# Recurrent retention and a channel mix on one core: block 2's layout, the place of the value weights, and a new order of pieces

## The chip, the core and the metric

The kernel runs on one core of a Trainium2 chip. Five engines work side by side, each through its own queue in order: TensorE (PE, matrix products; its weight loads are shown as PEld), VectorE (DVE), ScalarE (ACT), GpSimd (POOL) and SyncE (SP). Transfers are issued from the queues of POOL, SP and ACT and carried by 16 DMA engines. The metric is the time of one execution in microseconds on the device; lower is better. A profile is one execution taken by the hardware profiler.

## The reference, cut to what matters

Inputs: q, k, v of shape (4, 8, 768, 64): 4 batches, 8 heads, 768 tokens, 64 numbers a head. Then the weights of a channel mix, with 512 columns in and out and 1024 inside. All float32.

```python
# part 1, retention, each batch and head by itself
for t in range(S):
    state = gamma * state + outer(k[t], v[t])
    y[t] = scale * (q[t] @ state)
# part 2, with x = the heads of y side by side, 512 numbers a token
x_prev = x one token earlier (zero for the first)
xk = mu_k * x + (1 - mu_k) * x_prev
xr = mu_r * x + (1 - mu_r) * x_prev
k = max(xk @ w_k, 0);  v = k * k @ w_v
out = sigmoid(xr @ w_r) * v
```

## The kernel before, in words

The 768 tokens of a batch are cut into 3 blocks of 256, so there are 12 blocks, numbered 0 to 11; block n belongs to batch n // 3. Within a block the recurrence is done as products: scores of keys against queries, masked to be causal, times the values (inside the block), plus the queries times a carried state (from the blocks before). Each block's result is then mixed with its shifted self and goes through three projections.

The order of all work is written out by hand in one string, ORDER (lines 24 to 80). Each word is a piece: a code, numbers (block first, then parts), after "@" the PSUM banks that it writes, after "~" the engine (v DVE, a ACT, p POOL, s SP; pieces of TensorE have none). The kernel walks through the words and issues each at once, so the string sets the order of every engine's queue. The waits between engines follow from the tiles that the pieces share. Nothing is moved by a planner afterwards.

The codes that matter here (functions in brackets):

- lq, lk, lv (load): block n's q, k, v from memory; lq.0.0.2 is the part of block 0 for heads 0 to 3. POOL's loads of q and k turn float32 into float16. wk.h, wv.h, wr (load_wk, load_wv, load_wr): the projections' weights, wk and wv in two halves.
- cq, ck (cast): the first halves of block 0's q and k, loaded by SP as float32, to float16. vs (scale_v): v with the decay of each token.
- Tq, Tk (trans): transposes of q and k on TensorE. Eq, Ek (turned_q, turned_k): their copies out of PSUM.
- S (scores), M (masked, on DVE); C (state), U (summed), G (decayed): the carried state. I (inter_off) and J (inter_on): queries times carried state. Y (intra): masked scores times values.
- D (yout): result of a block to x transposed. dx (differ), t (weighed) and X (mixed): xk and xr (X.n.0.j and X.n.1.j, j a quarter of the 512).
- K (keys), Qa (relued), Qb (squared): first projection, its max with 0, its square. R (gate), s (opened): the sigmoid's projection, the sigmoid. V (values), O (result), st (store): second projection, product with the sigmoid, and the store of 128 tokens. V.n.tb.half reads half of wv. Vc, Oc and sc do the last 128 tokens in two column halves.
- z.c: products of zeros on TensorE that nobody reads. cm (masks), gy (powers), mu, mt, me: constants.

How a block's 256 tokens lie over partitions depends on the lists at the top. Blocks in HALF (6 to 11) use 64x64 tiles of TensorE. Blocks in WIDE (2 to 5, line 22) and HALF load k and v in two transfers of 128 tokens, 64 numbers a run (line 229); the others load 256 tokens in one transfer, two neighbouring tokens a run of 128 numbers (line 234). For WIDE blocks, scores take 64x128 tiles (line 330), the state and the values 128x64 tiles (lines 383 and 477). Blocks in neither list take 64x64 tiles for all three (lines 338, 394 and 488), twice as many products. Blocks in WHOLE (0 to 3) are transposed in 128x64 tiles (line 271), the others in 64x64 (line 277).

Two pieces of TensorE recur 120 times in all and are of one size, four products of 512 columns or eight of 256: K (48 pieces), R (24) and V (46, and two pieces Vc of the same length).

Buffers are rings: 4 for q and k in float16 and for v, 3 for masked scores and mixed inputs. A load waits until the block that held its buffer is done with it.

Of the kernel before, what the change touches and what calls it, by code (L numbers as in the profile page):

```python
# [34 lines left out]
X.1.1.1~v Qa.1.0~a t.0.1.0~a K.1.2@7 I.2@23 Qb.0.1~a Qa.1.1~a wv.0~p Qb.0.2~a Tq.4@01 Eq.4~a Y.2
Qa.1.3~a Qb.1.1~a X.0.1.3~v X.1.1.3~v R.1.1@4 Tk.4@01 Ek.4~a J.2 R.1.0@6 Qa.1.2~a s.1.0~a X.0.1.2~v
X.0.1.1~v X.0.1.0~v R.0.1@5 s.0.1~a s.1.1~a R.0.0@7 s.0.0~a S.4.1@01 Qb.1.0~a D.2~v dx.2~v X.2.0.2~v
X.2.0.0~v S.4.0@23 Tq.3@4 Eq.3~a X.2.0.1~v wv.1~p X.2.0.3~v Tk.3@7 lq.5~p Ek.3~a K.2.2@5 Qa.2.2~a
K.2.3@4 M.4.1~v M.4.0~v Qa.2.3~a Qb.2.3~a lk.6~p S.3.1@67 M.3.1~v S.3.0@01 vs.3~p C.3@23 U.3.0~a
Qb.2.2~a K.2.1@4 Qa.2.1~a K.2.0@2 Qa.2.0~a I.3@45 lq.6~p vs.4~v C.4@67 U.3.1~v X.2.1.1~v V.0.1.0@3  # L40
M.3.0~v V.1.0.0@2 G.3~a U.4.0~v I.4@01 X.2.1.3~v U.4.1~v J.3 Qb.1.3~a Y.4 Qb.2.0~a lk.5~p X.2.1.2~v
X.2.1.0~v Y.3 D.3~v dx.3~v V.0.0.0@7 V.0.1.1 O.0.1~v Tq.5@45 J.4 D.4~v dx.4~v R.2.0@6 Qb.2.1~a
V.0.0.1 O.0.0~v X.3.0.1~v Eq.5~a Qb.1.2~a V.1.0.1 X.3.0.2~v O.1.0~v Tq.6@01 Eq.6~a Tk.6@45 Ek.6~a
st.0.0~s lk.7~p st.1.0~s V.1.1.0@3 V.1.1.1 O.1.1~v s.2.0~a R.2.1@0 s.2.1~a lv.5~p X.3.0.0~v
X.3.0.3~v Tk.7@67 Ek.7~a G.4~a S.6@45 M.6~v Tk.5@23 Ek.5~a vs.5~v V.2.0.0@0 K.3.2@1 Qa.3.2~a K.3.0@6
S.5.0@23 M.5.0~v S.5.1@45 C.5@1 U.5.0~v K.3.3@7 Qb.3.2~a Qa.3.0~a lq.7~p K.3.7@6 Qa.3.3~a Qa.3.7~a
lv.6~p lq.8~p vs.6~v M.5.1~v V.2.0.1 st.0.1~s I.5@67 O.2.0~v st.2.0~s C.6@23 U.6.0~a U.6.1~v U.6.2~v
K.3.6@1 Qa.3.6~a lk.9~p X.3.1.3~v Y.5 Tq.7@45 Eq.7~a U.6.3~v X.3.1.2~v I.6@01 J.5 X.3.1.0~v D.5~v
X.3.1.1~v Qb.3.3~a G.6~a V.2.1.0@2 K.3.1@3 V.2.1.1 O.2.1~v Qb.3.7~a Qa.3.1~a Qb.3.1~a dx.5~v K.3.4@4
K.3.5@5 Qa.3.5~a X.5.0.0~v X.5.0.3~v R.3.1@2 s.3.1~a lv.7~p Qa.3.4~a X.5.0.1~v Qb.3.4~a R.3.0@5  # L50
R.4.0@2 s.3.0~a s.4.0~a Qb.3.0~a X.5.0.2~v vs.7~v K.5.2@4 S.7@67 st.1.1~s M.7~v Qb.3.5~a Y.6
Qb.3.6~a lv.10~p C.7@23 U.7.0~v X.5.1.1~v Qa.5.2~a K.5.0@5 R.4.1@6 Qa.5.0~a D.6~v s.4.1~a V.4.0.0@4
V.4.0.1 V.3.1.0@5 U.7.1~v Qb.5.0~a X.5.1.3~v U.7.2~v I.7@01 X.5.1.2~v U.7.3~v Tq.8@67 Eq.8~a
X.5.1.0~v O.4.0~v lv.8~p vs.8~v Qb.5.2~a lq.10~p lk.8~p Tk.8@23 Ek.8~a V.3.1.1 V.3.0.0@4 C.8@67
O.3.1~v st.2.1~s st.3.1~s Y.7 dx.6~v D.7~v Tq.10@23 V.3.0.1 Eq.10~a G.7~a dx.7~v X.6.0.2~v V.4.1.0@5
V.4.1.1 X.6.0.0~v R.5.0@0 R.5.1@1 K.5.3@2 Qa.5.3~a Qb.5.3~a O.3.0~v s.5.0~a K.5.1@4 X.6.0.1~v lq.9~p
lk.10~p Qa.5.1~a Qb.5.1~a lv.11~s s.5.1~a X.6.0.3~v K.6.3@2 Qa.6.3~a K.6.2@3 K.6.5@4 Qa.6.2~a
U.8.0~v Qa.6.5~a X.6.1.2~v V.5.0.0@0 st.3.0~s X.6.1.0~v K.6.4@1 Qa.6.4~a O.4.1~v U.8.1~v X.6.1.1~v
U.8.2~v I.8@45 S.8@67 Tk.10@23 Ek.10~a V.5.0.1 lv.9~p X.6.1.3~v vs.9~v K.6.6@1 Qb.6.2~a M.8~v
Qa.6.6~a Qb.6.5~a S.10@67 O.5.0~v Y.8 M.10~v D.8~v vs.10~v dx.8~v st.5.0~s st.4.0~s Tk.9@23 Ek.9~a  # L60
V.5.1.0@1 V.5.1.1 X.8.1.3~v vs.11~v O.5.1~v lk.11~p Qb.6.3~a Tk.11@23 Qb.6.4~a X.8.0.1~v X.8.0.3~v
lq.11~p Tq.11@67 Ek.11~a X.8.1.2~v Tq.9@45 Eq.9~a K.6.1@0 Qa.6.1~a Eq.11~a R.6.0@2 s.6.0~a K.6.7@4
R.6.1@5 s.6.1~a Qa.6.7~a C.9@23 S.11@67 X.8.0.0~v C.10@01 K.6.0@5 U.9.0~a Qa.6.0~a Qb.6.0~a U.9.1~v
X.8.0.2~v Qb.6.6~a U.9.2~v U.9.3~v G.9~v Qb.6.1~a R.7.0@4 s.7.0~a K.8.1@5 Qa.8.1~a K.8.0@3 Qa.8.0~a
# [733 lines left out]
```

## Time and profile before

| What | us |
|---|---|
| median of 3 runs | 154.2 (153.81 to 154.3) |
| the profiled execution, whole | 154.38 |
| its span, first to last instruction | 152.6 |
| PE busy | 144.1 |
| DVE busy | 128.7 |
| ACT busy | 100.6 |
| POOL busy | 55.3 |

The span is what the trace shows; the whole execution has some 1.8 us around it. In the views that follow, a row of the chain of waits has start, length and what was done then. A row of a timeline has start, length, engine, line, operation and tiles. A row of transfers has the tiles, the issuing queue, the count, the size and the median time from issue to landing. Rows of groups have busy time and mean length of one, then the engine's idle time before them. A row of windows has the stretch, its length, then for PE, PEld, DVE, ACT and POOL the busy time with the count of instructions, the granted clock, the DMA share and GB/s.

### The profile page before, as it was taken

To read this page: it belongs to the slowest core of one execution; us is meant where nothing else is said; L and a number is where in the kernel's file an instruction comes from. 1 tells how busy PE (TensorE), PEld (TensorE's weight loads), DVE (VectorE), ACT (ScalarE), POOL (GpSimd) and SP (SyncE) were. 2 spreads that over 40 slices of the span, in tenths; PEclk is the share of its full clock that TensorE was granted. 3 is DMA by queue.
4 is the path that set the end of the run, shared out by engine and by line. 5 is a ranking of instruction groups with operands and counts; after the bars stand their busy time and mean duration, and the time that the engine had idled before them with its cause. 6 is when DMAs were issued, how large, how long until landed. Compare 5 with 4: busy or idle time off the path is not lost.

```text
span 152.6 us, 5532 instructions
## 1 busy us (share of the span) xinstructions
PE 144.1 (94%) x2426; PEld 82.9 (54%) x2426; DVE 128.7 (84%) x214; ACT 100.6 (66%) x187; POOL 55.3 (36%) x65
## 2 busy tenths in 40 slices
PE   7977799999999999999999999899999999999990
PEld 3354487758655554547554655557555445744450
DVE  7876999999999999999999999999789999702240
ACT  3466979899934894979483889879405048997130
POOL 7954988579867109997600000000000000000000
PEclk9999999999999999999999999999999999999999
DMA  5999999999999999999999203220002050010435
GB/s 137 215 224 200 207 229 194 170 249 210 196 167 207 236 250 112 290 275 203 206 191 225 83 0 136 81 73 0 4 4 75 0 205 1 14 54 4 158 117 206
DMA packets 45624, 22.16 MB, mean 145 GB/s; under 512 B 37400, under 2 KB 41248, under 8 KB 45600
## 3 DMA queue, kind: packets, MB, share of 16 engines
q0 software_dynamic: 38704, 14.42, 74.0%
q1 hardware_dynamic: 6592, 7.21, 13.7%
q8 instruction: 19, 0.31, 0.8%
q10 hardware_dynamic: 304, 0.18, 0.5%
q14 instruction: 5, 0.04, 0.1%
HBM read 24.16 MB, written 6.29 MB: 200 GB/s over the span
## 4 chain that ended last, share of the span: by engine, by line
PE 91%; DVE 3%; ACT 2%; issue 1%; DVEq 0%
PE ps L623 27%; PE ps L581 14%; PE ps L611 14%; PE ps L571 14%; PE ps L701 4%; PE ps L277 3%; PE ps L440 2%; PE ps L271 2%; DVE a L353 2%; PE ps L330 1%; PE ps L477 1%; ACT qT L240 1%; PE ps L317 1%; PE ps L461 1%; PE ps L641 1%; PE ps L365 1%
## 5 line engine op out<-in xcount | busy, mean ns | idle before, releaser
L623 PE MATMUL ps<-wv,k2s 128*128 128x512 f16 x184 | 43.3, 380 | 0.0
L590 ACT ACTIVATE kr<-ps 128x512 f32<-128x512 f32 x48 | 27.4, 596 | 21.5 <-PE ps L581 11.1
L623 PEld LDWEIGHTS <-k2s 128*128 128x128 f16 x184 | 17.0, 98 | 19.3 <-ACT k2s L602 0.2
L629 DVE SCALAR_TENSOR_TENSOR os<-ps,rs 128x512 f32<-128x512 f32 x23 | 15.5, 685 | 12.4 <-ACT rs L617 7.1
L611 PE MATMUL ps<-wr,xr 128*128 128x512 f16 x96 | 23.5, 379 | 0.0
L581 PE MATMUL ps<-xk,wk 128*128 128x256 f16 x192 | 23.4, 273 | 0.0
L571 PE MATMUL ps<-xk,wk 128*128 128x512 f16 x96 | 22.9, 379 | 0.0
L229 POOL DMA_DIRECT2D k<-in_k_dram x20 | 17.9, 908 | 11.1 <-PE ps L383 6.8
L581 PEld LDWEIGHTS <-wk 128*128 128x128 f16 x192 | 18.3, 98 | 4.4 <-issue 0.2
L240 ACT COPY qT<-ps 128x1024 f16<-128x1024 f16 (+1 forms) x13 | 12.4, 951 | 9.2 <-PE ps L277 7.8
L557 DVE SCALAR_TENSOR_TENSOR xr<-dx,mu,xT 128x256 f16<-128x256 f32 (+1 forms) x32 | 18.0, 579 | 0.1
L617 ACT ACTIVATE rs<-ps 128x512 f32<-128x512 f32 x24 | 13.7, 594 | 6.1 <-DVE os L629 3.2
L229 POOL DMA_DIRECT2D v<-in_v_dram x18 | 16.0, 904 | 3.6 <-DMA wr<-in_moe_w_r_dram 1.9
L557 DVE SCALAR_TENSOR_TENSOR xk<-dx,mu,xT 128x256 f16<-128x256 f32 (+1 forms) x32 | 17.1, 581 | 0.2
L353 DVE TENSOR_TENSOR a<-ps,c_sb 128x1024 f16<-128x1024 f32 (+1 forms) x14 | 14.6, 1066 | 0.7 <-PE ps L338 0.4
L602 ACT ACTIVATE k2s<-kr 128x512 f16<-128x512 f32 x24 | 14.6, 626 | 0.2
L571 PEld LDWEIGHTS <-wk 128*128 128x128 f16 x96 | 9.1, 98 | 10.3
L611 PEld LDWEIGHTS <-xr 128*128 128x128 f16 x96 | 9.1, 98 | 10.2 <-DVE xr L557 0.3
L598 ACT ACTIVATE k2s<-kr 128x512 f16<-128x512 f32 x24 | 14.4, 625 | 0.3
L240 ACT COPY kT<-ps 128x1024 f16<-128x1024 f16 (+1 forms) x13 | 12.3, 944 | 2.9 <-PE ps L271 2.0
L528 DVE TENSOR_TENSOR dx<-xT 128x1024 f32<-128x1024 f32 x11 | 13.5, 1223 | 0.3
L252 DVE TENSOR_TENSOR vs<-v,csm_sb 128x1024 f16<-128x1024 f32 x10 | 12.2, 1219 | 0.2 <-DMA v<-in_v_dram 0.2
(74 smaller groups left out, 165.5 us busy)
## 6 DMA issues: line engine op xcount, KB each, us to landing
out_dram<-os SPq DMA_DIRECT2D x23, 256.0 KB, 3.0
v<-in_v_dram POOLq DMA_DIRECT2D x18, 256.0 KB, 7.3
q<-in_q_dram POOLq DMA_DIRECT2D x11, 256.0 KB, 7.8
k<-in_k_dram POOLq DMA_DIRECT2D x21, 128.0 KB, 8.9
v<-in_v_dram POOLq DMA_DIRECT2D x2, 512.0 KB, 7.1
wk<-in_moe_w_k_dram POOLq DMA_DIRECT2D x2, 512.0 KB, 11.2
wv<-in_moe_w_v_dram POOLq DMA_DIRECT2D x2, 512.0 KB, 9.7
wr<-in_moe_w_r_dram POOLq DMA_DIRECT2D x1, 512.0 KB, 9.3
```

The source lines that it names most:

```text
L229: e.dma_start(out=dst[:, :, i * D : i * D + D], in_=src[:, i * P : i * P + P].rearrange("h p d -> p h d"),)
L240: e.copy(out=out, in_=in_)
L353: nc.vector.tensor_tensor(out=a_full(n)[:, i, :, j0:j1], in0=pairs(banks("S", n, i, j0))[:, :, j0:j1], in1=(below if wide(n) else causal[: ...
L557: nc.vector.scalar_tensor_tensor(out=XM[w](k)[:, j, t0:t1], in0=DX(k)[:, j, t0:t1], scalar=mu[:, w * NCO + j : w * NCO + j + 1], in1=x[:, ...
L571: nc.tensor.matmul(banks("K", n, g), lhsT=wk16[:, co, g * P : g * P + P], rhs=XM[0](k)[:, co, :], start=(co == 0), stop=(co == NCO - 1),)
L581: nc.tensor.matmul(pz[:, i, :], lhsT=wk16[:, co, fo * P : fo * P + P], rhs=XM[0](k)[:, co, m * TM + t0 : m * TM + t1], start=(i == 0 and c ...
L590: nc.scalar.activation(out=kr, in_=banks("K", n, g, *u), func=AF.Relu)
L598: nc.scalar.activation(out=k2s[:, n % 3 : n % 3 + 2, g, :], in_=kr, func=AF.Square,)
L602: nc.scalar.activation(out=K2(n)[:, w * g : w * g + w, t0:t1], in_=kr.rearrange("p a t -> p (a t)").rearrange("p (i t) -> p i t", i=w), fu ...
L611: nc.tensor.matmul(banks("R", n, tb), lhsT=XM[1](k)[:, co, t : t + P], rhs=wr16[:, co, :], start=(co == 0), stop=(co == NCO - 1),)
L623: nc.tensor.matmul(banks("V", n, tb), lhsT=K2(n)[:, fo, tb * P : tb * P + P], rhs=wv16[:, fo, :], start=(fo == 0), stop=(fo == NFO - 1),)
L629: nc.vector.scalar_tensor_tensor(out=OS(2 * n + tb), in0=banks("V", n, tb), scalar=1.0 / (KSC * KSC), in1=RS(2 * n + tb), op0=ALU.mult, op ...
```

## The change

Five things change; all but two are in the string ORDER.

1. Block 2 leaves the list WIDE. Its k and v come in one transfer each, and its scores, state and values take 64x64 tiles: 32 score products instead of 16, 16 state products instead of 8, and 32 value products instead of 16.
2. The masks' constants are made in three parts at three places (cm.0, cm.1, cm.2) instead of all at the start.
3. On POOL's queue, q of block 2 stands ahead of wk, and wv.0, wr and wv.1 stand ahead of or among the loads of block 4 and ahead of those of block 3. Before, both parts of wv stood behind them.
4. Some pieces change engine: the first casts of block 0 and one eviction of its k go from ACT to DVE, vs.3 from POOL to DVE, U.0.0 from DVE to ACT.
5. All pieces stand in another order, with other PSUM banks. Of the products of zeros, four pieces of z.2 (eight products) are gone. Both transposes of block 2 stand ahead of the first K piece; before, Tq.2 stood behind the fourth. V pieces of blocks 0 and 1 come much earlier, and the first two stores with them.

```diff
-WIDE = (2, 3, 4, 5)
+WIDE = (3, 4, 5)
...
-cm gy.0~v mu~a lv.0~p lq.0.0.2~s lk.0.0.2~s ck.0.0.2~a cq.0.0.2~a z.12@6 Tq.0.0.2@0 Tk.0.0.2@1 gy.1~v
-z.1@2 mt@2 Ek.0.0.2~a Eq.0.0.2~a S.0.1.0.2@01 S.0.0.0.2@45 me~a lk.0.2.4~p Tk.0.2.4@2 Ek.0.2.4~a
-lq.0.2.4~p vs.0~v C.0@67 U.0.0~v Tq.0.2.4@3 Eq.0.2.4~a lq.1~p lk.1~p M.0.1.0.2~v z.2@2 S.0.1.2.4@23
-U.0.1~v lv.1~p lk.2~p I.0@01 S.0.0.2.4@67 M.0.0.2.4~v wk.0~p wk.1~p G.0~a z.2@6 Tq.1@6 Eq.1~a vs.1~p
-lq.2~p Tk.1@7 Ek.1~a M.0.0.0.2~v M.0.1.2.4~v Y.0 D.0~v t.0.0.3~a t.0.0.2~a t.0.0.1~a lv.2~p z.2@4
-S.1.1@23 M.1.1~v C.1@01 U.1.0~v z.2@4 I.1@23 S.1.0@67 X.0.0.1~v t.0.1.2~a X.0.0.2~v Tk.2@0 t.0.1.3~a
-t.0.0.0~a M.1.0~v X.0.0.0~v z.2@4 Y.1 t.0.1.1~a X.0.0.3~v Ek.2~a K.0.0@0 K.0.1@6 lq.4~p U.1.1~v
-G.1~a wr~p lk.4~p D.1~v dx.1~v X.1.0.2~v X.1.0.0~v K.0.2@1 Qa.0.0~a Qb.0.0~a Qa.0.2~a lq.3~p
...
+lv.0~p lk.0.2.4~p mu~a gy.0~v cm.2~v lq.0.2.4~p lq.0.0.2~s cq.0.0.2~v cm.0~v z.12@6 Tq.0.0.2@0
+Eq.0.0.2~a lk.0.0.2~s ck.0.0.2~v Tk.0.0.2@1 Ek.0.0.2~a mt@0 S.0.0.0.2@23 cm.1~v Tk.0.2.4@1 lq.1~p
+vs.0~v C.0@45 gy.1~v Tq.0.2.4@6 Eq.0.2.4~a M.0.0.0.2~v me~a U.0.0~a Ek.0.2.4~v U.0.1~v G.0~a
+S.0.1.0.2@23 M.0.1.0.2~v lk.1~p lv.1~p S.0.0.2.4@67 Tq.1@4 Eq.1~a I.0@01 S.0.1.2.4@23 lk.2~p lq.2~p
+M.0.0.2.4~v Tk.1@5 M.0.1.2.4~v Y.0 D.0~v Ek.1~a t.0.0.3~a S.1.0@23 M.1.0~v Tk.2@5 t.0.0.0~a wk.0~p
+wk.1~p lv.2~p vs.1~p C.1@01 U.1.0~v z.1@6 I.1@23 X.0.0.0~v t.0.0.2~a t.0.0.1~a S.1.1@67 wv.0~p wr~p
+Tq.2@0 X.0.0.1~v M.1.1~v z.2@4 Y.1 t.0.1.3~a Eq.2~a X.0.0.3~v t.0.1.0~a X.0.0.2~v D.1~v dx.1~v
+X.1.0.1~v X.1.0.2~v K.0.1@0 Ek.2~a K.0.0@6 X.1.0.0~v X.1.0.3~v Qa.0.0~a vs.2~v Qa.0.1~a Qb.0.1~a
+Qb.0.0~a U.1.1~v lq.4~p K.0.2@2 K.0.3@3 X.0.1.0~v X.1.1.3~v lk.4~p Qa.0.2~a Qb.0.2~a G.1~a K.1.2@0
+K.1.0@2 Qa.1.0~a S.2.0@67 M.2.0~v C.2@1 U.2.0~v V.0.1.0@5 Qa.1.2~a t.0.1.1~a X.1.1.0~v X.1.1.2~v
+t.0.1.2~a X.0.1.2~v K.1.3@4 Qa.1.3~a I.2@01 S.2.1@67 M.2.1~v V.0.0.0@2 K.1.1@4 X.1.1.1~v Qb.1.3~a
+Tq.4@67 X.0.1.3~v X.0.1.1~v Y.2 Qa.0.3~a D.2~v dx.2~v Qb.1.2~a Eq.4~a X.2.1.1~v X.2.0.0~v Qb.0.3~a
+X.2.1.2~v X.2.0.3~v Qa.1.1~a Qb.1.1~a R.0.0@3 s.0.0~a X.2.1.3~v X.2.0.1~v R.0.1@6 Qb.1.0~a s.0.1~a
+wv.1~p X.2.0.2~v Tk.4@01 R.1.0@4 R.1.1@3 s.1.1~a V.0.1.1 O.0.1~v st.0.1~s lv.3~p vs.3~v V.0.0.1
+O.0.0~v s.1.0~a Ek.4~a st.0.0~s K.2.2@4 K.2.1@5 Qa.2.1~a S.4.1@01 M.4.1~v Qa.2.2~a S.4.0@67 lk.3~p
+lq.3~p X.2.1.0~v C.3@23 U.3.0~a U.3.1~v Tk.3@5 Ek.3~a Tq.3@4 K.2.3@0 Eq.3~a lv.4~p M.4.0~v K.2.0@1
+vs.4~v Qa.2.3~a Qb.2.3~a Qa.2.0~a S.3.0@67 S.3.1@45 M.3.1~v Qb.2.2~a I.3@23 G.3~a V.1.0.0@0 V.1.0.1
+M.3.0~v O.1.0~v R.2.1@4 s.2.1~a C.4@67 U.4.0~v Y.3 lv.5~p lk.5~p Tk.5@45 vs.5~v I.4@01 J.3 V.1.1.0@6
+V.1.1.1 D.3~v dx.3~v lk.7~p Y.4 Qb.2.1~a Qb.2.0~a C.5@2 Ek.5~a Tk.7@45 Ek.7~a U.4.1~v G.4~a J.4
+D.4~v dx.4~v X.3.0.0~v R.2.0@3 s.2.0~a X.3.0.1~v V.2.0.0@7 lq.5~p lq.7~p Tq.7@01 Eq.7~a Tq.5@45
...
+Qa.5.3~a Qb.5.1~a V.4.0.0@1 V.4.0.1 Tk.9@23 Tk.8@45 lk.10~p Tk.10@67 lv.9~p V.5.1.0@0 Qb.5.3~a
...
-    def masks(e):
+    def masks(e, part):
         for out, col, op in (
-            (ident, 0, ALU.is_equal), (causal[:, 0], 1, ALU.is_ge), (causal[:, 1], 1, ALU.is_gt),
-            (step, 2, ALU.is_ge), (below, 0, ALU.is_ge),
-        ):
-            nc.vector.tensor_scalar(
+            ((ident, 0, ALU.is_equal),),
+            ((causal[:, 0], 1, ALU.is_ge), (causal[:, 1], 1, ALU.is_gt)),
+            ((step, 2, ALU.is_ge), (below, 0, ALU.is_ge)),
+        )[part]:
+            e.tensor_scalar(
```

More of the change, by code (lines that the diff above doesn't have):

```diff
@@ L35 @@
[L35 to L64, printed above, removed]
@@ new lines @@
+Qb.6.2~a X.8.0.2~v X.8.0.3~v K.6.7@5 S.9@23 Qa.6.7~a Qb.6.7~a I.9@67 S.10@01 M.9~v X.8.0.1~v
+X.8.0.0~v R.6.1@4 K.6.6@5 s.6.1~a R.6.0@4 s.6.0~a Qa.6.6~a Qb.6.6~a K.8.2@2 M.10~v K.8.0@3 lv.10~p
+vs.10~v lk.11~p X.8.1.2~v Qa.8.2~a Tq.11@45 Eq.11~a G.9~v C.10@01 U.10.0~v Y.9 D.9~v U.10.1~v
+K.8.1@2 Qa.8.0~a st.5.0~s Qb.6.1~a lv.11~s vs.11~v K.8.3@4 Qb.6.4~a U.10.2~v Qa.8.3~a U.10.3~v
+Qa.8.1~a Qb.8.0~a Qb.8.1~a G.10~v V.7.1.0@6 V.7.1.1 O.7.1~v C.11@23 U.11.0~v I.10@45 Tk.11@01
+V.6.0.0@7 Qb.8.3~a X.8.1.3~v U.11.1~v U.11.2~v Qb.8.2~a Ek.11~a X.8.1.1~v V.7.0.0@6 V.6.0.1 st.4.0~s
@@ new lines @@
+O.6.0~v S.11@23 I.11@01 X.8.1.0~v Y.10 M.11~v dx.9~v D.10~v dx.10~v V.7.0.1 X.9.0.0~v X.9.0.3~v
+V.8.0.0@7 V.8.0.1 R.8.1@2 V.6.1.0@3 V.6.1.1 R.8.0@4 st.4.1~s X.9.0.1~v O.6.1~v X.9.0.2~v s.8.1~a
+Y.11 D.11~v V.8.1.0@5 V.8.1.1 K.9.4@3 Qa.9.4~a s.8.0~a K.9.2@2 K.9.7@3 K.9.0@4 dx.11~v Qa.9.7~a
+Qb.9.4~a Qa.9.2~a X.11.0.0~v X.9.1.1~v X.11.0.2~v Qb.9.2~a Qa.9.0~a K.9.3@3 X.11.1.1~v Qa.9.3~a
+Qb.9.3~a K.9.1@0 X.11.0.3~v X.11.1.3~v X.11.0.1~v K.9.5@1 Qa.9.5~a K.11.1@4 K.11.3@3 st.6.1~s
+st.6.0~s Qb.9.5~a Qb.9.0~a K.11.2@1 Qa.11.3~a Qa.9.1~a Qb.9.1~a X.9.1.0~v Qa.11.1~a Qb.11.1~a
@@ new lines @@
+Qb.11.3~a X.11.1.2~v K.11.0@2 X.11.1.0~v R.11.0@0 X.9.1.3~v X.9.1.2~v R.10.0@3 K.9.6@4 Qa.9.6~a
+Qa.11.2~a O.8.1~v O.8.0~v R.9.1@7 st.8.1~s st.8.0~s Qb.9.6~a Qb.9.7~a R.10.1@4 V.9.0.0@1 s.9.1~a
+O.7.0~v st.7.0~s Qa.11.0~a Qb.11.0~a V.10.0.0@5 st.7.1~s R.9.0@2 s.9.0~a V.9.1.0@7 V.9.1.1 V.10.0.1
+O.9.1~v st.9.1~s s.10.0~a O.10.0~v V.11.0.0@3 V.9.0.1 O.9.0~v Qb.11.2~a st.9.0~s st.10.0~s s.11.0~a
+R.11.1@5 s.11.1~a V.10.1.0@2 V.10.1.1 V.11.0.1 s.10.1~a O.11.0~v O.10.1~v st.11.0~s st.10.1~s
+Vc.11.1.1@4 Vc.11.1.0@5 Oc.11.1.1~v Oc.11.1.0~v sc.11.1.1~a sc.11.1.0~s
```

33 lines of the change are left out of this document (16 added, 17 removed).

## The prediction

> **What bounds the kernel now.** I read the page first, then the chain of waits, then the loads on POOL's queue.
>
> ```profile
> PE 144.1 (94%) x2426; PEld 82.9 (54%) x2426; DVE 128.7 (84%) x214; ACT 100.6 (66%) x187; POOL 55.3 (36%) x65
> ...
> DVE  7876999999999999999999999999789999702240
> ...
> PEclk9999999999999999999999999999999999999999
> DMA  5999999999999999999999203220002050010435
> ...
> PE 91%; DVE 3%; ACT 2%; issue 1%; DVEq 0%
> ```
>
> TensorE holds 91% of the chain that ended last. DVE is as full as PE up to the 35th slice, and the DMA engines are full from the second slice to the 22nd. So there is one bound with two close followers: a microsecond saved counts only if it leaves PE's queue, and a delay of a load or of DVE counts only where PE has nothing else to do.
>
> The chain of waits (start, length, what) shows PE without a hole from the first projection piece on:
>
> ```profile
> 15.11 0.45 PE ps L338 x16
> ...
> 19.11 0.64 PE ps L488 x32
> ...
> 19.86 3.60 PE ps L581 x32
> 23.46 0.57 PE ps L271 x16
> ...
> 26.26 0.55 PE ps L330 x16
> ...
> 29.15 0.59 PE ps L477 x16
> ...
> 52.30 0.38 PE ps L277 x32
> 52.68 0.27 PE ps L317 x32
> ...
> 53.24 0.97 PE ps L623 x4
> 54.21 1.73 PE ps L571 x8
> ...
> 95.67 0.45 issue
> ```
>
> Before 19.86 PE works in short pieces with gaps; from there it runs K, R and V pieces of 0.865 us each (1.73 for two), 120 of them in both orders, with attention pieces between them. So the time is: start of the dense part, plus the fixed 120 pieces, plus small pieces, plus what each change of tile size costs, plus holes. Two rows give the price of such a change: the first transposes after a full piece take 0.38 where the scores of the same form and count behind them take 0.27, and the first V piece after a small run takes 0.97 instead of 0.865. That is 0.11 us per change, at entry and at exit.
>
> **The start, bound by loads.** In the changed order POOL's queue holds, before the two halves of wk, block 2's k as one load instead of two and block 2's whole q, which came behind wk before. The rows are issue (start, length) and, below each, that load's time to landing in the last column:
>
> ```profile
> 5.51 0.94 POOL L234 DMA_DIRECT2D v<-in_v_dram  x1
> ```
> ```profile
> v<-in_v_dram POOLq DMA_DIRECT2D x1, 512.0 KB, 8.0
> ```
> ```profile
> 8.12 0.82 POOL L733 DMA_DIRECT2D wk<-in_moe_w_k_dram  x1
> ```
> ```profile
> wk<-in_moe_w_k_dram POOLq DMA_DIRECT2D x1, 512.0 KB, 10.3
> ```
> ```profile
> 8.86 0.82 POOL L733 DMA_DIRECT2D wk<-in_moe_w_k_dram  x1
> ```
> ```profile
> wk<-in_moe_w_k_dram POOLq DMA_DIRECT2D x1, 512.0 KB, 12.1
> ```
> ```profile
> 15.43 0.95 POOL L234 DMA_DIRECT2D q<-in_q_dram  x1
> ```
> ```profile
> q<-in_q_dram POOLq DMA_DIRECT2D x1, 256.0 KB, 7.0
> ```
>
> Landings: v of block 1 at 13.5, wk's halves at 18.4 and 21.0, q of block 2 at 22.4. They land in order and back to back, so the spacings are prices: half of wk 2.5, a whole q 1.5. Between v (13.5) and the start of wk's first half (18.4 - 2.5 = 15.9) lies the split k: 2.4. In the new order that stretch holds k whole and q, 1.5 each as they have the same bytes: 3.0. So wk's second half lands at 21.0 + 0.6 = 21.6. Two halves of k can be issued in 1.8 (0.9 each, the row of POOL below), so 0.6 of the 2.4 may be a delay that belongs to that moment and not to the split; then it comes again, and the landing is 22.2. I take the middle, 21.9.
>
> The first K pieces of block 0 that read the second half (K.0.2, third in both orders) started at 19.86 + 2 x 0.9 = 21.6 before. After, they start at 22.0: **+0.4** (ends +0.1 and +0.7). What else is late in the start is hidden under this: DVE gets two casts of 512 columns and one eviction from ACT (about 0.6 each, half of a 1024-column scaling, whose row stands with the second rival) and gives one small sum of 0.4 to ACT, so +1.4, while this window shows 2.57 us of idle DVE (13.50 less 10.93) in the same stretch:
>
> ```profile
> sum 13.50, PE 10.57 PEld 6.88 DVE 10.93 ACT 9.18 POOL 9.60; mean PE 2.64 PEld 1.72 DVE 2.73 ACT 2.30 POOL 2.40
> ```
>
> Its cover is the wait for wk: the first K piece may start as late as 22.0 - 1.8 = 20.2, where it started at 19.86. Without that cover up to 1.0 would be added. The masks cut in three, gy.1 moved back and block 0's other load order cost nothing under the same cover. Eight of the eleven f16 zero products go; they stood in waits, so they give nothing back.
>
> **The dense part, from K.0.2 on.**
> - Tq.2 (0.57 at 23.46, its own entry in it, and 0.1 at its exit is counted next) is done before K in the new order, while PE waits anyway: **-0.57**.
> - Changes of tile size: counted along both orders from the first K piece, 24 runs of small pieces with 56 changes before, 23 with 51 after. Two of the 56 are Tq.2's. So three fewer: 3 x 0.11 = **-0.33**.
> - Block 2 in 64x64 tiles: 16 score products per half against 8, but 16 took 0.45 in one piece with its entry (15.11) and 2 x 8 wide ones 0.55 (26.26); the value products took 0.64 for 32 small against 0.59 for 16 wide. Both within 0.1, of both signs: **0**, range -0.1 to +0.1.
> - The 0.45 hole at 95.67 lies in the middle of 96 transposes in a row and waits for nothing that the profile shows. The new order also has 96 in a row (Tk.9, Tk.8, Tk.10). It may come again or not: I take **-0.2**, range -0.45 to 0.
> - vs.3 goes from POOL to DVE; its cost lies beside PE (below, a rival).
> - The end is the same work: a V piece, two Vc, two half results, two stores: 0.
>
> Sum: 0.4 - 0.57 - 0.33 - 0.2 = **-0.7**. The profiled execution took 154.38, its span and what lies around it, 0.18 over the median 154.2 of the runs. 154.38 - 0.7 - 0.18 = **153.5 us**.
>
> **Rivals.**
>
> *Loads without slack (slower).* PE waited for no load after 19.86 before. In the new order wv's halves and wr stand ahead of blocks 3 and 4, so each load lands just before its use. Counting from wk's landing at 21.9 to q of block 7: v2 1.7 (one whole v behind one whole k), wv and wr 3 x 2.5, four q at 1.5, seven pairs of half loads at 1.8 (two issues of 0.9):
>
> ```profile
> L229 POOL DMA_DIRECT2D k<-in_k_dram x20 | 17.9, 908 | 11.1 <-PE ps L383 6.8
> ```
>
> 1.7 + 7.5 + 6.0 + 12.6 = 27.8, landing at 49.7. PE arrives at Tq.7 after 25 full pieces (21.6), some 6.4 of small pieces and 21 changes (2.2): 22.0 + 30.2 = 52.2. The first two stores now go out near 36, in the middle of this, where the first was at 50. What stores do to the queue, by two neighbouring loads around which three stores were issued:
>
> ```profile
> 48.50 0.89 POOL L229 DMA_DIRECT2D v<-in_v_dram  x1
> ```
> ```profile
> v<-in_v_dram POOLq DMA_DIRECT2D x1, 256.0 KB, 7.1
> ```
> ```profile
> 49.38 0.90 POOL L234 DMA_DIRECT2D q<-in_q_dram  x1
> ```
> ```profile
> q<-in_q_dram POOLq DMA_DIRECT2D x1, 256.0 KB, 9.6
> ```
>
> 55.6 to 59.0 is 3.4 instead of 1.5: 0.6 a store, 1.3 for two, so landing at 51.0 and a slack of 1.2. It decides when the loads are over 1.2 later than these minimum prices (0.09 for each of the 14 half loads would do). A lag of 2.4 would give a wait of 1.2 and 154.7; up to 155.2 if the start is at its late end as well.
>
> *DVE becomes the bound (no change).* DVE gains one scaling of 1.2 there, 1.1 without the overlap of neighbours:
>
> ```profile
> 24.00:40.00 16.00, 15.98 (x282) 11.52 (x280) 15.85 (x23) 14.98 (x26) 12.67 (x15) 1.00 1.51 207
> ```
> ```profile
> L252 DVE TENSOR_TENSOR vs<-v,csm_sb 128x1024 f16<-128x1024 f32 x10 | 12.2, 1219 | 0.2 <-DMA v<-in_v_dram 0.2
> ```
>
> In this window DVE (third figure) was busy 15.85 of 16. If PE's mixed inputs wait for it, +1.1 comes back: 154.6. Against it: V pieces of blocks 0 and 1 are now early and can stand before what waits.
>
> *Loads at their early end (faster).* wk lands at 21.6, and the hole at 95.67 does not come back: 153.5 - 0.3 - 0.25 = 152.95.
>
> *The clock falls (slower).* The granted clock (PEclk) reads 9 tenths or more in every slice, and 1.00 in the window above. Without eight zero products of 512 columns (a quarter of a V piece, 0.22 each) and with Tq.2 (0.57) PE's 10.57 busy of 13.50 in the start becomes about 9.4, or 70%. If the gate closes, the small pieces and the first 3.4 us of K run at half speed: +1.7 at least, 155.2. The Trainium skill (TensorE: Matmul & The Clock Gate, part 1) states that one idle window of about 3.4 us throttles the clock to half. By that rule this change is safe, since no gap shown comes near 3.4 us; no run here shows how much partial idleness is too much.
>
> **How the numbers follow.** Forecast 0.50, loads at their early end 0.12, DVE bound 0.12, loads without slack 0.20, clock 0.06. The forecast's own range is 153.0 to 154.0. A difference of 0.3% (0.46 us) is about what a measurement can tell, so faster is below 153.74, slower above 154.66. Of the forecast 0.38 lies below and 0.12 within; early loads count as faster; DVE as within; of the late loads 0.17 slower and 0.03 within; the clock slower. Faster 0.50, same 0.27, slower 0.23. The range 152.7 to 155.2 takes in the early loads and the late ones.
>
> **What would show it.** Right: wk's second half lands at 21.6 to 22.2 and PE has a wait for it of 0.3 to 0.9 in front of K.0.2; from there PE has no wait over 0.3; 23 runs of small pieces; granted clock 1.00. Wrong: PE waits for q or k of blocks 5 and 7 between 45 and 53 us; waits for DVE's xk or a tiles between 40 and 110 us; K pieces of 1.7 us near 20; several holes put down to issue in the runs of transposes.

## The result, and the profile after

The changed kernel took 156.56 us (median of 6 runs, 156.06 to 158.4) against 154.25 for the kernel before in the same call: ratio 1.0144, 95% interval 1.0116 to 1.0172. It is slower by 1.4%; 153.5 was forecast, and the time lies above the range of 152.7 to 155.2. Below, a kernel's time is its ratio to the kernel before in the same call, and in us that ratio times 154.3 (156.5 for the changed kernel); the ratio is taken from undisturbed executions alone, which for the kernel with the load order mended are six of eleven (the other five took 157.1 to 160.0).

The profiled execution took 156.52, with a span of 154.7 against 152.6. Its page: busy time, slices, the queue of instructions, the chain by engine, one group.

```profile
PE 144.1 (93%) x2458; PEld 83.8 (54%) x2458; DVE 130.7 (84%) x217; ACT 100.0 (65%) x185; POOL 51.7 (33%) x62
...
PE   7989789999999799959999999999999999999991
...
PEclk9987999999999999999999999999999999999998
...
q8 instruction: 19, 0.31, 0.8%
...
PE 78%; DMA 9%; POOL 5%; ACT 3%; issue 2%; DVE 0%; ACTq 0%; POOLq 0%
...
L581 PE MATMUL ps<-xk,wk 128*128 128x256 f16 x192 | 22.9, 273 | 0.7 <-DMA wk<-in_moe_w_k_dram 0.7
```

TensorE is busy for 144.1 us, as before, with 32 products more. So the 2.1 us are time in which it stands. The busy time by stretches tells where (stretch, its length, PE busy, then PEld, DVE, ACT, POOL, granted clock, DMA share, GB/s); first the kernel before, then the changed one (in the stretches left out PE is busy throughout):

```profile
0.00:26.00 26.00, 21.99 (x382) 13.73 (x384) 21.99 (x52) 17.03 (x36) 20.14 (x26) 1.00 1.32 202
...
50.00:70.00 20.00, 20.00 (x307) 10.17 (x305) 19.70 (x29) 16.11 (x32) 12.18 (x15) 1.00 1.19 228
...
90.00:110.00 20.00, 19.55 (x524) 11.65 (x511) 18.41 (x29) 16.21 (x27) 0.00 (x0) 1.00 0.16 56
...
130.00:155.00 25.00, 18.54 (x106) 10.16 (x104) 6.57 (x12) 11.78 (x23) 0.00 (x0) 0.97 0.23 85
```
```profile
0.00:26.00 26.00, 21.91 (x370) 14.57 (x370) 22.57 (x54) 14.63 (x30) 18.13 (x24) 0.93 1.24 209
...
50.00:70.00 20.00, 17.45 (x361) 9.18 (x356) 19.13 (x25) 15.37 (x28) 11.68 (x14) 1.00 1.42 199
70.00:90.00 20.00, 19.63 (x457) 11.72 (x455) 17.84 (x31) 12.66 (x25) 8.65 (x10) 1.00 0.98 136
...
110.00:130.00 20.00, 19.84 (x298) 9.71 (x296) 19.06 (x32) 8.07 (x15) 0.00 (x0) 1.00 0.08 28
130.00:155.00 25.00, 21.28 (x123) 11.76 (x121) 9.87 (x18) 13.60 (x26) 0.00 (x0) 0.98 0.29 106
```

Idle time of TensorE is length less busy time. In the start it is 4.01 before and 4.09 after (+0.1). From 50 to 70 us it is nothing before and 2.55 after, from 70 to 90 nothing and 0.37, from 90 to 110 it is 0.45 before and nothing after, from 110 to 130 nothing and 0.16. The dense part thus loses 2.55 + 0.37 + 0.16 - 0.45 = 2.63. From 130 to the end of the span (152.6 and 154.7) 4.06 and 3.42 are idle: -0.64, since the span ends 3.0 us behind the last result (DVE's, at 151.74), where it ended 3.6 us behind it (at 148.99). Sum: 0.1 + 2.63 - 0.64 = 2.1.

The chain of waits of the changed kernel has the same places (start, length, what):

```profile
8.92 13.48 DMA wk<-in_moe_w_k_dram
22.40 0.05 issue
22.44 3.67 PE ps L581 x32
```
```profile
51.92 0.86 PE ps L623 x4
52.79 0.78 issue
53.57 0.71 PE ps L277 x64
...
68.61 0.27 ACT tg L240
68.89 0.19 issue
69.08 0.45 PE ps L277 x32
...
85.74 0.15 PE ps L277 x4
85.89 0.37 issue
86.27 0.94 PE ps L277 x92
```

K.0.2 starts at 22.44, when wk's second half is there. Three holes (stretches in which TensorE stands) follow, at Tq.7 (from 52.79), Tk.6 (up to 69.08) and Tk.9 (from 85.89). Two are put down to "issue", as the one at 95.67 before. The longest is put down to ScalarE. The list of waits of TensorE (who waited for whom, us in all, times, the longest) has them:

```profile
PE ps L277 <- ACT tg L240: 1.8, 1, 1.8
PE ps L277 <- issue: 1.2, 2, 0.8
```

That attribution is doubtful: in the program Tk.6 waits for the reading of R.3.0 by ScalarE (it frees the bank), which was over at 67.07, and TensorE went on at 69.08. The three holes are 0.78, 1.77 and 0.37 us of idle time, 2.92 in all, against the one of 0.45 before: +2.47 of the 2.63. The rest is a wait of 0.16 for ScalarE at K.9.3.

What the four holes have in common shows when the instructions of TensorE's program are counted, where every product is two (weight load and product). The instruction queue q8 moves 19 packets of 16,384 bytes in either kernel, and the packets lie some 256 of TensorE's instructions apart. Call 256 instructions, 128 products, a block. With the first block ending at instruction 182 of the program and one more every 256, each hole falls on a block end. (The trace shows each of the three fp32 zero products as two, so there 94 products stand ahead of the first block end; the holes have 94 + 128 x 13 products ahead of them in the kernel before, and 94 + 128 x 6, x 8 and x 11 in the changed one. The 94 holds in the runs with fewer fp32 products too.) Out of the trace (us, times of products are their starts):

```
hole at              block entered   packet for the next block   last product, next product
before, Tk.11        92.50           93.46 to 94.68              95.47   96.11
after,  Tq.7         47.06           50.95 to 52.14              52.41   53.57
after,  Tk.6         64.52           66.77 to 67.69              67.09   69.08
after,  Tk.9         81.39           83.84 to 84.80              85.68   86.27
```

In each, TensorE goes on 1.4 us after the packet's end, whatever it stood in front of. The packet for the next block starts some time after the block ahead of it is entered. So a block ends in a hole when TensorE gets through its 128 products in less than that time, plus 1 us for the packet, plus 1.4. That became the theory (the "fetch theory"). The rivals: ScalarE is late, as the profile's releaser says; the changed order makes loads late; the smaller tiles or the clock cost by themselves.

### The profile page after: what moved, and what is told of

Its sections match the earlier page's. It is cut to its first block, busy times and chain, and to the rows that moved or that the text cites. A ratio compares the mean times of both kernels' runs of the same rounds, so it can differ in the third digit from the quotient of the medians.

```text
span 154.7 us, 5597 instructions
## 1 busy us (share of the span) xinstructions
PE 144.1 (93%) x2458; PEld 83.8 (54%) x2458; DVE 130.7 (84%) x217; ACT 100.0 (65%) x185; POOL 51.7 (33%) x62
## 4 chain that ended last, share of the span: by engine, by line
PE 78%; DMA 9%; POOL 5%; ACT 3%; issue 2%; DVE 0%; ACTq 0%; POOLq 0%
PE ps L623 26%; PE ps L611 13%; PE ps L581 13%; PE ps L571 13%; DMA wk<-in_moe_w_k_dram 9%; PE ps L277 4%; PE ps L440 2%; POOL q L234 2%; POOL k L234 2%; ACT k2s L598 1%; POOL v L234 1%; PE ps L461 1%; ACT kr L590 1%; PE ps L317 1%; PE ps L641 1%
## 5 line engine op out<-in xcount | busy, mean ns | idle before, releaser
L581 PE MATMUL ps<-xk,wk 128*128 128x256 f16 x192 | 22.9, 273 | 0.7 <-DMA wk<-in_moe_w_k_dram 0.7
L571 PE MATMUL ps<-xk,wk 128*128 128x512 f16 x96 | 22.2, 379 | 0.2 <-ACT kr L590 0.2
L229 POOL DMA_DIRECT2D k<-in_k_dram x18 | 16.0, 910 | 13.8 <-PE ps L383 4.3
L229 POOL DMA_DIRECT2D v<-in_v_dram x16 | 14.5, 927 | 4.8 <-DMA wk<-in_moe_w_k_dram 2.4
L240 ACT COPY kT<-ps 128x1024 f16<-128x1024 f16 (+1 forms) x12 | 11.6, 976 | 3.4 <-PE ps L277 3.1
L252 DVE TENSOR_TENSOR vs<-v,csm_sb 128x1024 f16<-128x1024 f32 x11 | 13.4, 1218 | 0.0
```

The source lines that it names most:

```text
L229: e.dma_start(out=dst[:, :, i * D : i * D + D], in_=src[:, i * P : i * P + P].rearrange("h p d -> p h d"),)
L240: e.copy(out=out, in_=in_)
L571: nc.tensor.matmul(banks("K", n, g), lhsT=wk16[:, co, g * P : g * P + P], rhs=XM[0](k)[:, co, :], start=(co == 0), stop=(co == NCO - 1),)
L581: nc.tensor.matmul(pz[:, i, :], lhsT=wk16[:, co, fo * P : fo * P + P], rhs=XM[0](k)[:, co, m * TM + t0 : m * TM + t1], start=(i == 0 and c ...
```

## The experiments

**Other block ends with the order unchanged.** If the theory holds, the kernel before must get holes from products that do nothing, if they only shift the block ends. A first set put them into the start, in the place of fp32 zero products:

```diff
+    def pads(e, count):
+        z16 = zero.bitcast(F16)
+        for _ in range(count):
+            nc.tensor.matmul(banks("p", count)[0:W, 0:W], lhsT=z16[0:W, 0:W], rhs=z16[0:W, 0:W],
+                             start=True, stop=True, skip_group_check=True)
-... z.12@6 Tq.0.0.2@0 ...
+... z.4@6 p.64@6 Tq.0.0.2@0 ...
```

(with 128: p.128; in the changed kernel z.8 p.24 and z.4 p.104.)

> The kernel before, its order of pieces untouched, but for 8 of its first 12 zero products, in whose place stand 64 products of one 64x64 tile with 64 columns (on zeros, at the start, while PE has nothing else). Fetch theory: TensorE's program is read in blocks of 256 instructions (128 products), so all later block ends move 128 instructions forward in the order; they then fall on Tk.5, Tq.10, Tk.9 and Tq.9, where products are small, and PE stands there 0.6 to 2 us each: 2.5 to 4.5 us slower than before, 156.7 to 158.7 us. Order theory (the holes come from ScalarE or a load that the changed order makes late): the order is that of before, so within 0.5 us of it.

> As the run with 64, but 128 small products, 256 instructions, so that the block ends fall on the very places of before. Fetch theory: no change beside the start, within 0.5 us of before, with the hole at Tk.11 of before (0.6 us) and no other. If the small products themselves or the missing zero products cost time (clock, start), this run is slower than before and so much of the run with 64 is to be taken off.

> The kernel after with 24 small products in place of 4 zero products at the start: block ends 48 instructions earlier in the order. Fetch theory: the holes at Tq.7 (0.84 us), Tk.6 (1.9) and Tk.9 (0.57) go, smaller ones come at Tk.7 (0.3 to 0.9) and Y.7 (0.7 to 1.3); 0.5 to 1.5 us faster than after, 155.0 to 156.0 us. ScalarE theory (Tk.6 waits for the copy of s.3.0, as the releaser says): the hole at Tk.6 stays, within 0.3 us of after.

> The kernel after with 104 small products in place of 8 zero products: block ends 208 instructions earlier, which is 48 later in the next block. Fetch theory: holes at Tk.6 (1.7 to 2.3 us), Tq.10 (0.7 to 1.3), Tk.9 (0.6 to 1.2), K.8.3 (0.3): 1.0 to 2.3 us slower than after, 157.5 to 158.9 us. ScalarE theory: within 0.3 us of after.

Measured: 162.48 (its profiled execution), 162.2 (ratio 1.0512, 1.0458 to 1.0566), 160.8 (1.0418, 1.0372 to 1.0464) and 163.5 (1.0599, 1.0533 to 1.0666). The control with 128 failed its expectation, so none of these times tells anything: all products lay in one quadrant and went one behind the other, 0.055 us each, 7.0 us for 128, and the whole start moved. The places of the holes can still be read (here and below, a hole's size is from the start of the last product to the start of the next, some 0.2 to 0.4 us more than its idle time): with 64 at Tq.8 (0.85), Tq.10 (2.66) and Tq.9 (1.60), with 24 at Tk.7, C.6, C.7 and Y.7 (0.95, 1.06, 0.46, 2.30), with 104 at Tq.7, Tk.6 and Tq.10 (0.50, 3.70, 3.13), all on shifted block ends. With 128 no hole falls on a block end; the one at Tk.11, which the theory had back, did not come.

**The same, clean.** The products now go round the four quadrants and stand behind Tq.2, in the dense part, so that the start stays as it was:

```diff
+            a, u = low(x % 2), low(x // 2 % 2)
+            nc.tensor.matmul(banks("p", count)[u, x % 2, 0:W], lhsT=z16[a, u], rhs=z16[a, 0:W], ...)
-... Tq.2@1 X.1.1.2~v ...
+... Tq.2@1 p.64@45 X.1.1.2~v ...
-... Tk.4@01 Ek.4~a J.2 R.1.0@6 ...
+... Tk.4@01 Ek.4~a J.2 p.64@56 R.1.0@6 ...      (the second run only)
```

> The kernel before, every piece in its place; 64 products of 64x64 tiles with 64 columns, on zeros and going round the four quadrants so that they run beside one another, stand behind Tq.2 (PE has no idle time there, so they cost their own 0.6 to 0.9 us). Behind them the block ends of TensorE's program fall 128 instructions earlier in the order: Tk.5, Tq.7, Tq.8, Tq.10, Tk.9, Tq.9. Fetch theory: holes there, at Tq.10 the longest (1.4 to 2.7 us), 2.5 to 4.5 us in sum; with the products' own time 157.0 to 159.5 us. Order theory (holes come from what another order makes late on ScalarE or in the loads): the products' own time alone, 154.8 to 155.1 us.

> The same 64 products behind Tq.2 and 64 more behind J.2: 256 instructions in all, so that from block 4 on the block ends fall on the places of before (Tk.11 the only hole, 0.6 us). Fetch theory: the products' own time alone, 1.2 to 1.8 us, 155.4 to 156.0 us: twice the products of the run with 64, and faster than it. If products put in there cost by their delay of everything behind them, this run is slower than the run with 64.

> 22 such products behind Tq.2, 44 instructions. Fetch theory: no block end falls where products are too dense, the hole at Tk.11 of before (0.6 us) goes; own time 0.25 to 0.4 us: 153.6 to 154.1 us, at most as long as before. Order theory: 154.4 to 154.7 us.

> The kernel after with 24 such products ahead of S.2.0, 48 instructions. Fetch theory: no holes at Tq.7, Tk.6 and Tk.9 (1.16, 1.98 and 0.58 us between products there in after); others at Tk.7 (0.4 to 0.9), C.6 (up to 1.0), Y.7 (0.7 to 1.3); own time 0.3 us: 155.2 to 156.4 us. ScalarE theory: the hole at Tk.6 stays, 156.6 to 157.0 us.

Measured: 161.5 (1.0465, 1.0417 to 1.0513), 159.3 (1.0325, 1.0266 to 1.0383), 155.6 (1.0082, 1.0057 to 1.0107) and, for the changed kernel with 24, 159.5 (1.0337, 1.0291 to 1.0383). The stands in the chain of waits of the first (behind 50 us), the second (behind 28 us) and the last (50 to 106 us):

```profile
53.93 0.46 issue
...
77.50 0.55 issue
...
81.22 2.47 issue
...
102.77 1.13 issue
```
```profile
31.87 2.30 issue
...
100.76 0.65 issue
```
```profile
72.08 0.67 issue
...
78.42 0.80 issue
...
83.20 2.21 issue
```

With 64, the holes are at Tk.5, Tq.8, Tq.10 and Tq.9, four of the six places named, the longest at Tq.10 (2.66), and one more block end, at S.4.0 (0.86), lies ahead of the rows shown. With 128 they are all gone, and Tk.11 has its hole back; the order of the pieces is the same in both and in the kernel before. So no change of the order is needed for a hole: where the block ends fall is enough. The run with 128 is faster than the one with 64, as only this theory said. All four are slower than their ranges, though. With 64 (157.0 to 159.5 was expected) the clock was at half for 3.41 us behind the hole at Tq.10. With 128 (155.4 to 156.0) the second group of 64 products hit a block end itself (31.87, 2.30), and the clock was at half for 3.41 us behind that. The run with 22 lost the hole at Tk.11 as forecast, but got others at Tk.8 (1.11) and V.4.1.1 (0.63). The one with 24 in the changed kernel was to be faster and is slower: Tq.7, Tk.6 and Tk.9 are free as forecast, but the holes at C.7, Tq.8 and Y.7 (0.86, 0.99 and 2.40) are longer than those that went. There the packets came 3.3 to 4.0 us after their block was entered, where the packets of the same number in the changed kernel had come after 1.1 to 2.5.

That lag is the second half of the matter. Over 18 traces (all but the one with 128 products at the start and one execution of 783 us) the packet starts 2.4 us after the first product of the block ahead (median of 149, nine in ten under 4.1) between 26 and 85 us, where loads flow, and 1.0 (median of 56) between 95 and 112 us, where few or none do.

**The cost by itself.** 384 products that do nothing behind J.2, where loads flow, and 512 behind the last piece:

> The disputed cost by itself: the kernel before with 384 products of 64x64 tiles (zeros, four quadrants in turn, 0.0084 to 0.017 us each, 1.1 to 2.2 us for 128) behind J.2, where loads flow, and 512 behind the last piece, where none do. Fetch theory: TensorE runs 128 of them and then stands, over and over, at instructions 182 + 256 k; 3.3 to 3.6 us from one stand to the next at the end, where no loads flow, and 4 to 7 us behind J.2 while they do. Without such a limit both trains run through, 3.2 to 6.5 and 4.3 to 8.6 us in one piece.

```profile
30.98 0.92 PE L718 MATMUL ps<-zero 64*64 64x64 f16 x88
35.01 1.92 PE L718 MATMUL ps<-zero 64*64 64x64 f16 x128 [3.11 <-issue]
40.93 1.93 PE L718 MATMUL ps<-zero 64*64 64x64 f16 x128 [4.00 <-issue]
47.67 0.75 PE L718 MATMUL ps<-zero 64*64 64x64 f16 x40 [4.82 <-issue]
...
172.23 1.24 PE L718 MATMUL ps<-zero 64*64 64x64 f16 x128 [3.18 <-issue]
175.68 1.92 PE L718 MATMUL ps<-zero 64*64 64x64 f16 x128 [2.22 <-issue]
179.41 0.59 PE L718 MATMUL ps<-zero 64*64 64x64 f16 x28 [1.81 <-issue]
```

The timeline of TensorE: 128 products, a stand, 128 products, a stand. From start to start it takes 5.9 and 6.7 us while loads flow (35.01, 40.93, 47.67), within the 4 to 7 forecast, and 3.45 and 3.73 with none (172.23, 175.68, 179.41), near the 3.3 to 3.6 forecast. The granted clock was at half in most of both groups of such products (from 33.77 to 50.84 and from 173.72, where 128 products took 1.92 us); but TensorE went on 1.35 to 1.74 us behind a packet at each stand, so the clock did not set these times. They are the price of one block when its products are small: 128 products of long pieces last 28 us (0.865 for four), 128 transposes 1.4 (64 took 0.71 above).

**The hole at Tk.6.** Between the block ends in front of it and at it stand Tq.6, I.5, S.7, R.3.0, Y.5, C.6 and J.5, one long piece among small ones. The first run moves two gates in, with their readings:

```diff
-R.3.0@4 s.3.0~a Y.5 ... J.5 Tk.6@45 ... R.4.1@6 V.4.1.0@7 R.3.1@0 dx.5~v s.3.1~a s.4.1~a V.4.1.1
+R.3.0@4 s.3.0~a R.3.1@5 s.3.1~a R.4.1@6 s.4.1~a Y.5 ... J.5 Tk.6@45 ... V.4.1.0@7 dx.5~v V.4.1.1
```

The second run (with R.3.1 in bank 7) leaves the two readings behind the square of K.3.4 on ScalarE.

> The kernel after with two gate pieces of block group 3 and 4 (R.3.1 and R.4.1, 8 products of 128x512) moved from behind Tk.6 to ahead of Y.5, and their two sigmoid readings with them; nothing added or left out. Fetch theory: 1.9 us of long products now stand in the block of 256 instructions that ended too early at Tk.6; the hole there (1.98 us between products) closes but for 0 to 0.5 us, a new one of up to 0.9 us may come at V.3.1.1: 0.8 to 1.9 us faster than after, 154.6 to 155.8 us. ScalarE theory (Tk.6 waits for ScalarE, as the releaser says): Tk.6 now waits for one sigmoid reading more of 0.6 us ahead of it, no gain or up to 0.6 us slower, 156.5 to 157.2 us.

> As the run with R.3.1 and R.4.1 ahead of Y.5, but their sigmoid readings stand behind the square of K.3.4 on ScalarE, so that the squares for V.4.1.0 are not delayed. Fetch theory: no hole over 0.5 us at Tk.6 or J.5, no wait of V.4.1.0 for ScalarE; 1.0 to 2.0 us faster than after, 154.5 to 155.5 us. ScalarE theory: the hole at Tk.6 is back (1.5 us or more), since ScalarE does the same work ahead of it as in after.

Measured: 155.9 (1.0105, 1.0073 to 1.0137) and 156.2 (1.0126, 1.0070 to 1.0183). In both the hole at Tk.6 is gone; the block end now lies in J.5, where no stand is left. In the second, ScalarE does in front of Tk.6 what it does in the changed kernel, so the releaser that the profile named had no part in it. But the time hardly fell (156.5 without the moves; 154.6 to 155.8 and 154.5 to 155.5 were expected). In the second run's profile TensorE's idle time behind 26 us is 3.08 us, just as in the changed kernel. The stand at Tk.9 grew (1.11 us idle, 0.37 in the changed kernel), and the moves made waits of their own, which the list of waits shows:

```profile
PE ps L623 <- ACT rs L617: 1.1, 1, 1.1
...
PE ps L611 <- ACT qT L240: 0.4, 1, 0.4
```

V.4.1.0 waits for the reading that frees its bank (1.1), R.3.1 for Eq.6 (0.4).

**The load order and the sum.**

```diff
-lk.2~p lq.2~p ... wk.0~p wk.1~p lv.2~p ... Tq.2@0 ... K.0.2@2 K.0.3@3
+lk.2~p ... wk.0~p wk.1~p lq.2~p lv.2~p ... K.0.2@2 K.0.3@3 Tq.2@4
```

(Eq.2 behind Qa.0.2.) The second run has this and the second version of the gates; the third has R.3.1 in bank 5, R.4.1 just ahead of J.5, and the square of K.3.1 ahead of the others.

> The kernel after with the load of q of block 2 issued behind both halves of wk, as before, and Tq.2 behind K.0.3. Load term: the second half of wk lands 1.0 to 1.5 us earlier (22.40 in after), K.0.2 starts at 21.2 to 21.6 in place of 22.44, less 0.57 us for Tq.2, which stands on the path again: 0.3 to 0.8 us faster than after, 155.8 to 156.3 us. If the load's late landing is hidden by the holes behind it (block ends come at fixed times after the fetch before): within 0.3 us of after.

> The same together with the load of q of block 2 behind wk and Tq.2 behind K.0.3. If load order and holes are the loss: 153.2 to 154.6 us, about the time of before or under it, with the hole at Tq.7 (0.8 us) left, and that at Tk.9 (up to 0.6). If the gains don't add (the next block end takes what one mends): 154.8 us or more.

> Load order mended (q of block 2 behind wk, Tq.2 behind K.0.3) and the gates R.3.1 and R.4.1 ahead of Tk.6, R.3.1 in a bank that is free (5), R.4.1 just ahead of J.5, the square of K.3.1 ahead of the other squares so that V.4.1.0 does not wait. If load order and holes are the loss: no wait of R.3.1, at most 0.3 us at V.4.1.0, no hole at Tk.6; 1.0 to 1.9 us faster than the version with the bad bank, 153.2 to 154.6 us, level with before. If the time stays at 155 us or more, a part of the loss is of another cause.

Measured: 155.2 (1.0058, 1.0031 to 1.0084), 155.6 (1.0086, 1.0046 to 1.0126) and 156.0 (1.0112, 1.0073 to 1.0152). The load order alone gives back 1.3 us, more than the 0.3 to 0.8 forecast, and no wait for wk is left: wk's halves land at 17.76 and 20.28 (18.43 and 20.93 in the kernel before). The work from S.2.0 on starts hardly earlier than in the changed kernel (25.94 against 26.04), so most of the gain came later; in its profile the hole at Tk.9 and the wait at K.9.3 are missing. The gains do not add. In the second run's profile the stands at block ends are down to 0.26 us, but the waits at V.4.1.0 and R.3.1 (1.12 and 0.37) are there as above. The third run has no hole at Tk.6 and no wait at V.4.1.0, as forecast, but stands elsewhere, which its list of waits puts down to VectorE:

```profile
PE ps L277 <- DVE dx L528: 0.9, 1, 0.9
...
PE ps L611 <- DVE a L346: 0.6, 1, 0.6
```

The first of these rows is a block end again, at Tq.7: the packet had landed 1.46 us before, and the reading that Tq.7 needs by the program (D.4) was over at 53.57 where TensorE went on at 54.88. With Tk.9 the stands at block ends are 1.64 us. The second row is a true wait for VectorE, at R.4.0; one of 0.36 at I.7 follows. The expectation said that at 155 us or more a part of the loss has another cause. At 156.0 that holds for this version: it has those waits for VectorE, and in its profile (an execution of 157.65 us) the clock was at half for 3.41 us from 18.6 on. No version beat the kernel before, so it is not shown that the whole 2.1 us can be won back by closing the holes.

**Block 2 wide again**, the order of after:

```diff
-WIDE = (3, 4, 5)
+WIDE = (2, 3, 4, 5)
-... Y.2 Qa.0.3~a ...
+... Y.2 J.2 Qa.0.3~a ...
```

> The kernel after with block 2 wide again (k and v loaded in two parts, scores in 64x128 and state and values in 128-row tiles as in before), all else in the order of after: undoes one part of the change. 32 products fewer, so block ends behind block 2 fall 64 instructions later in the order; Tq.7, Tk.6 and Tk.9 are not block ends any more, but S.7, R.3.1, C.8, Tk.8 are. Fetch theory: no holes at Tq.7, Tk.6, Tk.9; at C.8 and Tk.8 0.6 to 1.3 us each. The split loads delay wk by up to 0.9 us. In sum 156.5 to 158.5 us. Theory that the smaller tiles cost by themselves: 0.5 us or more faster than after, with the holes where they were.

> Block 2 wide again in the order of after, once more for a profile. Fetch theory: stands at block ends among S.7, R.3.1, Y.6, C.8 and Tk.8 (the longest of 0.6 to 2.7 us), none at Tq.7, Tk.6 and Tk.9; 158 to 160 us.

Measured: 159.0 (1.0301, 1.0242 to 1.0360) and 158.1 (1.0246, 1.0173 to 1.0319); 156.5 to 158.5 was expected of the first, 158 to 160 of the second. The first run's profile is of an execution of 783 us and is left aside. In the second's, the holes at Tq.7, Tk.6 and Tk.9 are gone, and TensorE stands at the block ends R.3.1 (1.72 between products; the profile names VectorE) and C.8 (2.56), both named beforehand:

```profile
PE ps L365 <- issue: 2.4, 1, 2.4
PE ps L611 <- DVE t L418: 1.3, 1, 1.3
```

So undoing this part does not bring the time back: with 32 products fewer the block ends fall on other places that are worse. The theory that the smaller tiles cost by themselves asked for 0.5 us less and the old holes, and neither came; beside the new holes a smaller cost of the tiles could not be seen.

**The clock.** The changed kernel's granted clock was half in one stretch of the start. Six zero products of 512 columns put back into the waits there:

```diff
-Ek.0.0.2~a mt@0 ... S.0.0.2.4@67 Tq.1@4 ... Y.0 D.0~v ... z.1@6 I.1@23
+Ek.0.0.2~a z.1@6 mt@0 ... S.0.0.2.4@67 z.2@4 Tq.1@4 ... Y.0 z.2@4 D.0~v ... z.2@6 I.1@23
```

> The kernel after with six f16 zero products of 128x512 put back in the waits of the start (one ahead of mt, two ahead of Tq.1, two behind Y.0, one more ahead of I.1); block ends fall 12 instructions earlier. Clock theory: the clock stays at 1.0 in the start, in most runs, and the time falls by 0.5 us or more, to 155.0 to 156.0 us. Fetch theory with wk: the clock may well stay at 1.0, but K.0.2 still starts at 22.0 to 22.5, when wk is there, the holes are at Tq.7 or R.2.0 (0.4 to 1.0), J.5 (1.2 to 1.9), V.4.0.1 or Tk.9 (0.3 to 0.7): 156.0 to 156.8 us.

> The same with q of block 2 loaded behind wk and Tq.2 behind K.0.3. No wait for wk at K.0.2; clock 1.0 in the start; the holes as in the run with the zero products: 154.4 to 155.4 us. If the clock had no part in the run with the load order alone: the same time as that run, within 0.4 us.

Measured: 155.9 (1.0103, 1.0064 to 1.0142) and, with the load order too, 156.4 (1.0139, 1.0082 to 1.0195). Stretches as above, of the changed kernel and of the run with the zero products:

```profile
7.03:10.44 3.41, 2.32 (x81) 1.72 (x80) 3.15 (x6) 1.76 (x6) 3.41 (x5) 1.00 1.79 183
10.44:13.86 3.42, 3.42 (x72) 2.75 (x75) 2.31 (x4) 2.66 (x8) 0.50 (x2) 0.50 1.49 251
```
```profile
6.84:10.25 3.41, 2.69 (x81) 1.85 (x78) 3.27 (x6) 1.67 (x5) 3.41 (x5) 1.00 1.58 152
10.25:13.66 3.41, 3.02 (x90) 2.23 (x90) 2.27 (x4) 2.92 (x9) 0.34 (x1) 1.00 1.47 256
```

The clock stays at 1.00. The time falls by 0.6 us, into the range of the clock theory (155.0 to 156.0), but with intervals that overlap, and the profile does not bear that theory out: K.0.2 still waits for wk and starts at 22.31, S.2.0 at 25.96 where it was 26.04, so by S.2.0 the clock in the start is worth 0.1 us. The holes are on the block ends named, though not of the sizes named: R.2.0 (1.82), J.5 (0.81) and V.4.0.1 (1.54). The version with the load order as well missed its range (154.4 to 155.4): it has no wait for wk and a clock of 1.00, but the block ends lie as in the run with the zero products, and TensorE stood 2.37 us at R.2.0.

Over the 18 traces, 55 gaps between starts of products of more than 0.6 us lie behind 26 us; 45 of them are at block ends, and in every one TensorE went on 1.25 to 1.74 us after a packet had landed. At no block end behind 26 us did it go on sooner than 1.25 us after its packet.

## Why the prediction was wrong

- *The hole at 95.67: it "waits for nothing that the profile shows", and "It may come again or not", -0.2, range -0.45 to 0.* This is the step that failed. The hole was the one sign of a limit, the fetch of TensorE's program, that the sum did not have. I looked for its cause at its own place, 96 transposes in a row, and let its recurrence be a matter of chance. The cause is how fast the 256 instructions in front of it go by, so every other order gets its own set of holes. The term measured +2.47 (0.45 before, 2.92 after). Between the two profiles -0.7 was forecast and +2.1 came, an error of 2.8; this term has 2.67 of it. The start and the changes of tile size, which were to bring -0.5 and cost 0.1, have 0.6, the wait at K.9.3 has 0.16, and the end took 0.64 off. The text did name "several holes put down to issue in the runs of transposes" as what would show it wrong, but gave it no price and no chance.
- *wk lands at 21.9, K.0.2 at 22.0: +0.4.* The direction was right, the size not: landing at 22.40, K.0.2 at 22.44 (22.09 to 22.44 in the three profiles with this load order in which it waits for wk). wk's two halves landed 3.35 apart (19.05 and 22.40) where 2.5 was taken. In the first run with the gates moved, of the same load order, they landed 2.53 apart (19.51 and 22.04); why is open.
- *Tq.2 ahead of K: -0.57.* It did move into the wait. Both terms together were to bring -0.17; by S.2.0 (26.04, against 25.94 with the old load order and Tq.2 behind K.0.3, the same work) they cost +0.1.
- *Three fewer changes of tile size: -0.33; block 2: 0.* Nothing of the first shows: busy time is the same, 144.1, and idle time alone makes up the difference in the dense part. Nothing speaks against block 2's 0 either, but the 32 products count as 64 instructions, and these move every block end behind them, which the sum gave no price.
- *The end: 0.* It measured -0.64, by the last store, behind the last result.
- *Rivals.* Loads without slack: q of block 7 landed at 50.9, within the 49.7 to 51.0 worked out, and TensorE was there at 52.79 (52.2 worked out, with 21 x 0.11 taken as 2.2 where it is 2.3). Tq.7 (53.57) waited for the fetch instead; but loads have a part, since the packets start later while they flow. The 155.2 of this rival has 0.2 that its terms (1.2 and 0.3) do not give. DVE bound: not in the changed kernel; it shows in the third version with both mends, by 0.59 and 0.36. The clock: it fell in the start, as that rival said, and was back before K started at 19.79; so the price set on it, 1.7, was not paid. The rule named there (TensorE: Matmul & The Clock Gate, part 1, in the Trainium skill: one idle window of about 3.4 us) is not what the trace shows: the stretch in front of the drop was 2.32 of 3.41 busy. All of the slower cases ended at 155.2; the fetch was in none.
